# Pooled attention and GELU MLP: keys of later batches turned by a transposing DMA instead of by TensorE

## The chip, the cores and the metric

The kernel runs on one core of a Trainium2 chip. The metric is the device time of one execution in microseconds (us). A core has five engines that each work through a queue of their own in program order: TensorE (PE, matmuls), VectorE (DVE), ScalarE (ACT), GpSimd (POOL) and SyncE (SP, which here only issues DMAs). POOL issues DMAs too. An instruction that waits holds up everything behind it in its own queue.

## The reference

```python
batch, n_heads, seq, head_dim = (8, 8, 576, 64)

def _attn_ref(q, k, v):
    B, H, S, D = q.shape
    pool = 8
    Sp = S // pool                                   # 72 pools
    scale = 1.0 / np.sqrt(D)
    k_p = k.reshape(B, H, Sp, pool, D).mean(axis=3)
    v_p = v.reshape(B, H, Sp, pool, D).mean(axis=3)
    scores = scale * np.matmul(q, k_p.transpose(0, 1, 3, 2))
    scores = scores - np.max(scores, axis=-1, keepdims=True)
    attn = np.exp(scores)
    attn = attn / (np.sum(attn, axis=-1, keepdims=True) + 1e-09)
    return np.matmul(attn, v_p)

def _moe_ref(x, w_in, w_out):
    h = x @ w_in                                     # 4608x512 @ 512x2048
    g = 0.5 * h * (1.0 + np.tanh(sqrt(2/pi) * (h + 0.044715 * h**3)))
    return g @ w_out                                 # 4608x2048 @ 2048x512

x = attn_out.transpose(0, 2, 1, 3).reshape(B * S, H * D)
out = _moe_ref(x, w_in, w_out)
```

Keys and values are averaged over groups of eight positions, so every head has only 72 keys. Inputs and output are f32; the kernel computes in bf16 with f32 sums.

## The kernel before, in words

The 4608 rows of x are worked off in nine groups g of 512 rows (NG = 9). A batch has 576 rows, so group g needs the attention of batches 0 to g at most; the attention of batch nb = g + 1 is computed inside stage g, between the matmuls of the MLP. After an opening part for batch 0, the main loop (L415 to L508) runs one stage for each g:

1. First half (L457 to L470): 64 matmuls with w_in (`p1_mm`, L321), the GELU of each of 16 column tiles `fo` on ACT (L326). A table `plan` (L438) says after which `fo` the preparing steps for batch nb are issued: the sums over eight positions on DVE (L136), the move of the last pooled v rows (`v_moves`, L148), and the transposes of the pooled keys on TensorE with their copies (`trans_k`, L169, L176, L184).
2. Second half (L496 to L505): 64 matmuls with w_out (`p2_mm`, L329). At the positions `pos` (L483) attention steps of batch nb are put between them: scores (`qk`, L224), exponentials on ACT (L231), the product with v (`av`, L244), the normalisation (`norm`, `mult`). The first `qk` stands at position 6, the first `av` at position 14. After 16 matmuls a tile of output is copied by DVE into an `osb` buffer (L334) and stored by four DMAs on SP (L339).

The keys of a batch are loaded in `kts` as 576 pooled rows over 128 partitions, four to a partition, and a fifth column that takes the last 64 k rows and, in its lower half, the last 8 pooled rows of v. So the pooled keys are not separated by heads; the five transposes and the copies out of PSUM sort them. `kTs[b][0]` and `kTs[b][1]` hold them for the two halves c of the queries: one fills partitions 0 to 63, the other 64 to 127, with zeros elsewhere, since a transposed q tile carries an even and an odd position in its two halves of partitions.

The data of batch g + 2 are asked for in stage g (`load_next`, L419 to L425, called at L428 or L473): POOL issues the load of q (cast to bf16), SP a transposing DMA of q (`trans_q_dma`, L213), then a tiny POOL copy into `gate` (L423) makes POOL wait until that transpose has landed, and POOL issues the loads of k and v. The copy is there only for this wait. Nothing else holds POOL back, so after the v loads of a stage it goes straight on to the q load of the next stage. `qs`, `qT`, `kts`, `vts` and `vps` have two buffers each, used by turns.

SP's queue holds in a stage, in this order: the transposing DMA of q (batch g + 2), the v move (batch nb), 16 stores.

Of the kernel before, what the change touches and what calls it, by code (L numbers as in the profile page):

```python
# [8 lines left out]
F32 = mybir.dt.float32  # L9
BF16 = mybir.dt.bfloat16  # L10
# [8 lines left out]
def kernel(  # L19
# [9 lines left out]
    nc = tc.nc  # L29
    B, H, S, D = q.shape  # L30
    Sp = S // 8
# [11 lines left out]
    KR = 4  # L43
# [4 lines left out]
    consts = ctx.enter_context(tc.tile_pool(name="consts", bufs=1))  # L48
    qp = ctx.enter_context(tc.tile_pool(name="qp", bufs=2))
    bp = ctx.enter_context(tc.tile_pool(name="bp", bufs=2))  # L50
    ep = ctx.enter_context(tc.tile_pool(name="ep", bufs=2))
    gpool = ctx.enter_context(tc.tile_pool(name="gp", bufs=1))
    opool = ctx.enter_context(tc.tile_pool(name="op", bufs=6))
    psp = ctx.enter_context(tc.tile_pool(name="ps", bufs=1, space=bass.MemoryType.PSUM))


# [5 lines left out]

    vts = [consts.tile([128, 4, 512], F32, name=f"vt{i}") for i in range(2)]

    kts = [consts.tile([128, KR + 1, 512], F32, name=f"kt{i}") for i in range(2)]

    def load_k(b, engs):
        rows = k[b].rearrange("h (j l) d -> (h j) (l d)", l=8)
        main = rows[0:128 * KR].rearrange("(p r) c -> p r c", r=KR)
        n = KR // len(engs)  # L70
        for i, eng in enumerate(engs):
            eng.dma_start(out=kts[b % 2][:, i * n:(i + 1) * n], in_=main[:, i * n:(i + 1) * n])  # L72
        engs[0].dma_start(out=kts[b % 2][64:128, KR], in_=rows[128 * KR:])  # L73
        rows = v[b].rearrange("h (j l) d -> j h (l d)", l=8)
        engs[-1].dma_start(out=kts[b % 2][0:64, KR], in_=rows[64:])

    def load_v(b, engs):
        rows = v[b].rearrange("h (j l) d -> j h (l d)", l=8)
        for i in range(2):
            engs[i % len(engs)].dma_start(out=vts[b % 2][64 * i:64 * i + 64], in_=rows[0:64, 4 * i:4 * i + 4])  # L80

    def load_q(b, i0=0, i1=2):
        if b not in qs:
            qs[b] = qp.tile([128, 2, T * D], BF16, name="qb")
        nc.gpsimd.dma_start(  # L85
            out=qs[b][:, i0:i1],
            in_=q[b].rearrange("(i h) (p t) d -> (h p) i (t d)", i=2, t=T)[:, i0:i1])
# [24 lines left out]
    gate = consts.tile([1, 2], BF16, name="gate")  # L112
# [2 lines left out]
    xT = consts.tile([128, KO, N], BF16, name="xT")  # L115

    kTs = [[consts.tile([128, H, Sp], BF16, name=f"kT{i}{e}") for e in range(2)] for i in range(2)]
    kps = [consts.tile([128, KR + 2, D], BF16, name=f"kp{i}") for i in range(2)]

    vps = [consts.tile([Sp, H, 2, D], BF16, name=f"vp{i}") for i in range(2)]  # L120
# [14 lines left out]
    def add(o, a, b):  # L135
        nc.vector.tensor_tensor(out=o, in0=a, in1=b, op=ALU.add)  # L136

    def k_steps(b, c=slice(0, KR + 1)):


        t = kts[b % 2]
        return [lambda: add(t[:, c, 0:256], t[:, c, 0:256], t[:, c, 256:512]),
                lambda: add(t[:, c, 0:128], t[:, c, 0:128], t[:, c, 128:256]),
                lambda: add(kps[b % 2][:, c], t[:, c, 0:64], t[:, c, 64:128])]

    def v_moves(b):

        nc.sync.dma_start(out=vps[b % 2][64:Sp, :, 0], in_=kps[b % 2][0:64, KR])  # L148

    def v_steps(b):  # L150
# [35 lines left out]
    def trans_k(b, bank):  # L186
        trans_k_mm(b, bank)
        for e in range(2):
            trans_k_copy(b, e, bank)
# [17 lines left out]
    def trans_q(b, i, t0, n, bank, eng):  # L207
        trans_q_mm(b, i, t0, n, bank)
        trans_q_copy(b, i, t0, n, bank, eng)

    def trans_q_dma(b):
        qTs[b] = bp.tile([128, 2, TP, 128], BF16, name="qT")
        nc.sync.dma_start_transpose(out=qTs[b].rearrange("p i t c -> p (i t) c"),  # L213
                                    in_=qs[b].rearrange("p i c -> p (i c)"))
# [6 lines left out]
    def qk(b, c, pr, bank):  # L221
        for e in range(2):
            h = 2 * pr + e
            nc.tensor.matmul(out=PS[:Sp, bank + e, :CH].rearrange("j (t p) -> j t p", p=32),  # L224
                             lhsT=kTs[b % 2][c][:, h],
                             rhs=qTs[b][:, h // 4, :, h % 4 * 32:h % 4 * 32 + 32],
                             start=True, stop=True)

# [65 lines left out]
    def act_set(name):  # L294
        nc.scalar.preload_act_table_set(name)  # L295
# [27 lines left out]
    def gelu(g, fo):  # L323
        if g not in gTs:
            gTs[g] = gpool.tile([128, FO, GROUP], BF16, name="gT")
        nc.scalar.activation(out=gTs[g][:, fo, :], in_=PS[:, h_bank(g, fo), :], func=ACT.Gelu_apprx_tanh)  # L326
# [80 lines left out]
    nc.vector.memset(kTs[1][1], 0.0)  # L407
    for w in vps:
        nc.vector.memset(w, 8.0)

    for fo, ko in [(fo, ko) for ko in range(2) for fo in range(4)]:
        p1_mm(0, fo, ko)
# [2 lines left out]
    for g in range(NG):  # L415
        nb = g + 1 if g + 1 < B else None
        act_set(GELU_SET)

        def load_next():  # L419

            load_q(g + 2)
            trans_q_dma(g + 2)
            nc.gpsimd.tensor_copy(out=gate, in_=qTs[g + 2][0:1, 1, TP - 1, 0:2])  # L423
            load_k(g + 2, [nc.gpsimd])
            load_v(g + 2, [nc.gpsimd])  # L425

        if 0 < g and g + 2 < B:
            load_next()  # L428


        side = {fo: [] for fo in range(FO)}
        if nb is not None:
            kk = k_steps(nb)
            tk = [lambda: trans_k(nb, 4)]
            kk.append(lambda: v_moves(nb))
            vv = v_steps(nb)
            if g:
                plan = {2: kk[:1], 3: kk[1:], 7: vv[:1], 8: vv[1:], 9: tk}  # L438
            else:
                tq = [lambda a=a, i=i: trans_q(nb, *a, (5, 6, 7, 5)[i], nc.vector) for i, a in enumerate(QG)]  # L440

                kk.insert(1, lambda: (nc.vector.memset(vts[1][:, 0, 0:1], 0.0), load_v(1, [nc.sync])))
                plan = {0: kk, 12: tq[:1], 13: tq[1:2] + tk, 14: tq[2:3], 15: tq[3:] + vv}
            for fo, what in plan.items():
                side[fo] += what

        if g == 0:
            first = [(fo, ko) for ko in (2, 3) for fo in range(4)]  # L450
        else:
            late = 3
            rest = [fo for fo in range(4) if fo != late]
            first = [(fo, ko) for ko in range(3) for fo in rest]
            first += [(late, ko) for ko in range(3)]
            first += [(fo, 3) for fo in rest + [late]]
        for fo, ko in first if g + 1 < NG else ():  # L457
            p1_mm(g, fo, ko)
        for fo in range(FO):
            if g + 1 == NG:  # L460

                for c0, c1, turned in ((0, 384, False), (384, GROUP, True)):
                    for ko in range(KO):
                        p1_mm(g, fo, ko, c0, c1, turned)
            elif fo >= 4:
                for ko in range(KO):
                    p1_mm(g, fo, ko)
            gelu(g, fo)
            for s in side[fo]:
                s()  # L470

        if g == 0:
            load_next()  # L473


        todo = {}

        def at(m, f, *a):
            todo.setdefault(m, []).append((f, a))

        if nb is not None:
            act_set(EXP_SET)
            pos = (6, 14, 20, 27, 34, 41, 48, 55, 61)  # L483
            for i in range(len(ORDER) + 1):
                if i < len(ORDER):
                    at(pos[i], qk, nb, *ORDER[i], 2)
                if i:
                    a = (nb, *ORDER[i - 1], 4 + 2 * ((i - 1) % 2))
                    at(pos[i], av, *a)
                if i < len(ORDER):  # L490
                    at(pos[i], expo, nb, *ORDER[i], 2)
                if i:
                    at(pos[i], norm, *a)
                    at(min(pos[i] + 9, 62 if i < len(ORDER) else 65), mult, *a)

        seq = [(r, fo) for r in range(4 if g + 1 < NG else 3) for fo in range(FO)]  # L496
        if g == 0:

            seq[:32] = [(r, 4 * f4 + f) for f4 in range(4) for r in range(2) for f in range(4)]
        for m, (r, fo) in enumerate(seq):  # L500
            for f, a in todo.pop(m, []):
                f(*a)
            p2_mm(g, r, fo, o_bank(g, r))
            if fo == FO - 1:
                store(g, r, o_bank(g, r))  # L505
        for m in sorted(todo):
            for f, a in todo[m]:
                f(*a)  # L508
    for c0, bank in ((0, o_bank(g, 3)), (256, 4)):
# [5 lines left out]
        b, col = divmod(N - 128, S)  # L515
        t = col % CH // 32
        rows = out[b * S:(b + 1) * S].rearrange("(p t e) d -> e p t d", t=TP, e=2)
# [31 lines left out]
```

## Time and profile before

| what | value |
|---|---|
| time, median of 3 runs | 326.68 us (326.46 to 327.2) |
| the profiled execution | 326.68 us, span 324.9 us |
| TensorE / ScalarE / VectorE / GpSimd busy | 96% / 68% / 45% / 10% of the span |
| one stage, g = 1 to 6 | 31.85 us (for instance 127.71 to 159.56) |
| L321 and L329 matmuls on the chain that ended last | 37% and 38% |
| kt sums on DVE (L136), 128x1280, 128x640, 128x320 | 1493, 825, 491 ns |
| key transposes (L169) on the chain | 0.28 us a batch |
| POOL idle at the gate L423 | 151.2 us in 6 waits |
| q transpose by DMA, issue to landing | 4.6 us |

The span is cut by the profile into 40 slices; "the chain" follows the work that ended last backwards through what released it. In rows of a timeline the first number is the start in us from the beginning of the span, the second the length; in square brackets stands the idle time before, and what ended it. A row of SPq or POOLq is a DMA's issue. In rows of groups the numbers after the first bar are the busy time in us and the mean of one instruction in ns, those after the second the idle time before them. In a row of windows, the stretch and its length are followed by the busy time (and instruction count) of PE, PEld (weight loads), DVE, ACT and POOL, then the granted clock of TensorE (1.00 is full), the mean busy share of the DMA engines, and GB/s. In rows of DMA issues the last number is the median time from issue to landing.

### The profile page before, as it was taken

The page shows a single profiled execution, that of the slowest core. Times are in us where ns is not written, and L with a number is a line of the kernel's source. Part 1 is how long each engine was busy: PE and PEld are TensorE (multiplying, and loading weights), DVE is VectorE, ACT ScalarE, POOL GpSimd, SP SyncE. Part 2 cuts the span into 40 slices and gives each one's busy share as a digit, 9 for nine tenths or more (in the row PEclk, how much of TensorE's full clock was granted, in tenths as well). Part 3 has the DMA queues.
Part 4 walks back from the last instruction along what each step waited for, and adds up shares of the span by engine and source line. Part 5 has one row for each costly group of instructions (what it writes and reads, how often), then busy time and mean ns, then how long its engine had stood idle before and what let it go on. Part 6 is the DMA issues. An engine that isn't in the chain of part 4 may idle for free.

```text
span 324.9 us, 4442 instructions
## 1 busy us (share of the span) xinstructions
PE 311.8 (96%) x1621; PEld 167.6 (52%) x1621; DVE 145.8 (45%) x297; ACT 219.3 (68%) x402; POOL 31.3 (10%) x60
## 2 busy tenths in 40 slices
PE   8999919999999999999999999999999999999995
PEld 3555504555555555555555555555555554466544
DVE  4774434682568156805680577067616401200011
ACT  1677516976997799779877987798779873043300
POOL 7110004004000400220031002100000000000000
PEclk9999978999999999999999999999999999999999
DMA  7999955985925881598159527932002201210022
GB/s 230 257 282 217 246 106 192 247 186 160 225 75 108 228 201 38 108 265 161 48 124 259 138 57 97 262 81 67 1 10 57 65 0 34 65 32 2 0 54 76
DMA packets 30533, 41.11 MB, mean 127 GB/s; under 512 B 17904, under 2 KB 18160, under 8 KB 29616
## 3 DMA queue, kind: packets, MB, share of 16 engines
q0 software_dynamic: 7456, 24.38, 32.4%
q1 hardware_dynamic: 22424, 15.14, 19.3%
q10 hardware_dynamic: 632, 1.31, 1.2%
q8 instruction: 12, 0.20, 0.3%
q14 instruction: 9, 0.07, 0.1%
HBM read 36.70 MB, written 9.44 MB: 142 GB/s over the span
## 4 chain that ended last, share of the span: by engine, by line
PE 84%; DMA 11%; DVE 1%; POOL 1%; issue 0%; SPq 0%; DVEq 0%; POOLq 0%
PE PS L329 38%; PE PS L321 37%; DMA kt<-in_v_dram 7%; PE PS L244 4%; DMA vt<-in_v_dram 4%; PE PS L224 4%; DVE vt L136 1%; PE PS L169 1%; DVE kt L136 0%; POOL w_in_b L104 0%; POOL qb L85 0%; SPq L80 0%; POOL kt L72 0%; POOL kt L73 0%; DVE vp L136 0%
## 5 line engine op out<-in xcount | busy, mean ns | idle before, releaser
L321 PE MATMUL PS<-xT,w_in_b 128*128 128x512 bf16 (+2 forms) x640 | 137.9, 375 | 0.0
L329 PE MATMUL PS<-w_out_b,gT 128*128 128x512 bf16 (+1 forms) x592 | 137.8, 376 | 0.0
L326 ACT ACTIVATE gT<-PS 128x512 bf16<-128x512 f32 x144 | 81.7, 603 | 56.7 <-PE PS L321 56.7
L321 PEld LDWEIGHTS <-w_in_b 128*128 128x128 bf16 x640 | 72.1, 114 | 60.4
L329 PEld LDWEIGHTS <-gT 128*128 128x128 bf16 x592 | 58.0, 98 | 56.2 <-issue 1.8
L334 DVE COPY osb<-PS 128x512 f32<-128x512 f32 x35 | 24.2, 691 | 113.1 <-PE PS L329 112.8
L262 DVE TENSOR_TENSOR xT<-PS,rc 64x288 bf16<-64x288 f32 x112 | 51.0, 455 | 31.1 <-ACT rc L254 28.8
L231 ACT ACTIVATE e<-PS 72x576 bf16<-72x576 f32 x64 | 40.8, 644 | 11.4 <-PE PS L224 10.6
L244 PE MATMUL PS<-e,vp 72*128 72x288 bf16 x112 | 23.6, 291 | 6.9 <-DVE vp L136 6.8
L251 ACT ACTIVATE ld<-PS 64x288 f32<-64x288 f32 x56 | 22.8, 407 | 8.0 <-PE PS L244 6.6
L224 PE MATMUL PS<-qT,kT 128*72 128x288 bf16 x128 | 26.1, 289 | 0.9 <-ACT qT L203 0.6
L254 ACT ACTIVATE rc<-ld 128x288 f32<-128x288 f32 x56 | 24.8, 443 | 1.8
L295 ACT ACT_TABLE_LOAD x17 | 21.8, 1283 | 3.6 <-issue 3.3
L252 ACT ACTIVATE ld<-PS 64x288 f32<-64x288 f32 x56 | 22.5, 402 | 1.4
L224 PEld LDWEIGHTS <-kT 128*72 128x72 bf16 x128 | 14.4, 114 | 15.0 <-issue 1.3
L136 DVE TENSOR_TENSOR kt<-kt 128x1280 f32<-128x1280 f32 (+5 forms) x18 | 18.9, 1047 | 6.3 <-DMA kt<-in_k_dram 3.3
L136 DVE TENSOR_TENSOR vt<-vt 128x1024 f32<-128x1024 f32 (+1 forms) x16 | 15.3, 956 | 7.6 <-DMA vt<-in_v_dram 7.3
L176 DVE COPY kT<-PS 64x288 bf16<-64x288 bf16 (+2 forms) x48 | 13.2, 322 | 8.0 <-PE PS L169 7.9
L244 PEld LDWEIGHTS <-vp 72*128 72x128 bf16 x112 | 11.1, 100 | 10.5 <-DVE vp L136 7.1
L423 POOL COPY gate<-qT 1x2 bf16<-1x2 bf16 x6 | 1.0, 174 | 151.2 <-DMA qT<-qb 151.2
L345 PE MATMUL PS<-idle 128*128 128x512 bf16 x33 | 11.1, 487 | 1.5 <-DVE idle L125 1.2
L80 POOL DMA_DIRECT2D vt<-in_v_dram x12 | 7.6, 652 | 0.1
(45 smaller groups left out, 79.7 us busy)
## 6 DMA issues: line engine op xcount, KB each, us to landing
out_dram<-osb SPq DMA_DIRECT2D x140, 64.0 KB, 1.7
kt<-in_k_dram POOLq DMA_DIRECT2D x7, 1024.0 KB, 5.8
vt<-in_v_dram POOLq DMA_DIRECT2D x12, 512.0 KB, 9.5
qb<-in_q_dram POOLq DMA_DIRECT2D x7, 576.0 KB, 12.8
w_in_b<-in_moe_w_in_dram POOLq DMA_DIRECT2D x2, 1024.0 KB, 16.7
w_out_b<-in_moe_w_out_dram POOLq DMA_DIRECT2D x4, 512.0 KB, 22.6
vt<-in_v_dram SPq DMA_DIRECT2D x3, 512.0 KB, 10.6
kt<-in_k_dram POOLq DMA_DIRECT2D x7, 128.0 KB, 5.9
```

The source lines that it names most:

```text
L136: nc.vector.tensor_tensor(out=o, in0=a, in1=b, op=ALU.add)
L224: nc.tensor.matmul(out=PS[:Sp, bank + e, :CH].rearrange("j (t p) -> j t p", p=32), lhsT=kTs[b % 2][c][:, h], rhs=qTs[b][:, h // 4, :, h % ...
L231: nc.scalar.activation(out=e, in_=PS[:Sp, bank:bank + 2, :CH], func=ACT.Exp, scale=1.0 / 64.0)
L244: nc.tensor.matmul(out=PS[:, bank + x, :CH], lhsT=window(vps[b % 2], 2 * pr + x), rhs=e[:, x, :], start=True, stop=True)
L251: nc.scalar.activation(out=ld[0:64], in_=PS[64:128, bank, :CH], func=ACT.Ln)
L252: nc.scalar.activation(out=ld[64:128], in_=PS[0:64, bank + 1, :CH], func=ACT.Ln)
L254: nc.scalar.activation(out=rc, in_=ld, func=ACT.Exp, scale=-1.0)
L262: nc.vector.tensor_tensor(out=xT[rows, pr, col:col + CH], in0=PS[rows, bank + x, :CH], in1=rc[rows], op=ALU.mult)
L321: nc.tensor.matmul(out=out, lhsT=w, rhs=x, start=(ko == 0), stop=(ko == KO - 1))
L326: nc.scalar.activation(out=gTs[g][:, fo, :], in_=PS[:, h_bank(g, fo), :], func=ACT.Gelu_apprx_tanh)
L329: nc.tensor.matmul(out=PS[:, bank, c0:c1], lhsT=gTs[g][:, fo, r * 128:(r + 1) * 128], rhs=w_out_b[:, fo, c0:c1], start=(fo == 0), stop=(fo ...
L334: nc.vector.tensor_copy(out=osb, in_=PS[:, bank])
```

## The change

Batches 0 to 2 are prepared as before. For batch 3 and later (`KX = 3`):

- k is loaded with the 72 pools of a head on 72 partitions and the eight heads side by side (`load_k_dma`); the last eight pooled rows of v go to partitions 96 to 127 in two small loads.
- The sums (`k_steps_dma`) run over 8 x 256, 8 x 128 and 8 x 64 elements on 72 partitions and write bf16 into `kz`, whose 16 blocks of 128 columns are one for each head and half: in block e = 0 the pooled key stands in columns 0 to 63, in block e = 1 a copy of it in columns 64 to 127. The rest stays zero.
- A transposing DMA on SP (`trans_k_dma`) turns `kz` into `kx`, and `qk` reads its weights from there. The five transposes, the eight copies and their place in `plan` are gone for these batches.
- `v_moves` becomes two DMAs of four pools each.
- `load_next` for stages g of 2 and later is no longer called at the start of the stage but behind `trans_k_dma` after `fo` = 0, and begins with one more tiny copy into `gate`, out of `kx` of the coming batch. So POOL asks for q, and afterwards k and v, only when the key transpose has landed. `v_moves` follows `load_next`, after `fo` = 1.
- `osb` has five buffers instead of six, `kts` has eight columns instead of five, and POOL clears `kz` once.

SP's queue in stages 2 to 5 is then: transposing DMA of kz, transposing DMA of q (batch g + 2), two v moves, 16 stores. In stage 6 there is no q transpose.

```diff
--- before.py
+++ after.py
@@ -50,7 +50,7 @@
     bp = ctx.enter_context(tc.tile_pool(name="bp", bufs=2))
     ep = ctx.enter_context(tc.tile_pool(name="ep", bufs=2))
     gpool = ctx.enter_context(tc.tile_pool(name="gp", bufs=1))
-    opool = ctx.enter_context(tc.tile_pool(name="op", bufs=6))
+    opool = ctx.enter_context(tc.tile_pool(name="op", bufs=5))
     psp = ctx.enter_context(tc.tile_pool(name="ps", bufs=1, space=bass.MemoryType.PSUM))
 
 
@@ -62,7 +62,9 @@
 
     vts = [consts.tile([128, 4, 512], F32, name=f"vt{i}") for i in range(2)]
 
-    kts = [consts.tile([128, KR + 1, 512], F32, name=f"kt{i}") for i in range(2)]
+
+    kts = [consts.tile([128, H, 512], F32, name=f"kt{i}") for i in range(2)]
+    KX = 3
 
     def load_k(b, engs):
         rows = k[b].rearrange("h (j l) d -> (h j) (l d)", l=8)
@@ -74,6 +76,12 @@
         rows = v[b].rearrange("h (j l) d -> j h (l d)", l=8)
         engs[-1].dma_start(out=kts[b % 2][0:64, KR], in_=rows[64:])
 
+    def load_k_dma(b):
+        nc.gpsimd.dma_start(out=kts[b % 2][0:Sp], in_=k[b].rearrange("h (j l) d -> j h (l d)", l=8))
+        rows = v[b].rearrange("h (j l) d -> j h (l d)", l=8)
+        for y in range(2):
+            nc.gpsimd.dma_start(out=kts[b % 2][96:128, y], in_=rows[64 + 4 * y:68 + 4 * y])
+
     def load_v(b, engs):
         rows = v[b].rearrange("h (j l) d -> j h (l d)", l=8)
         for i in range(2):
@@ -115,6 +123,8 @@
     xT = consts.tile([128, KO, N], BF16, name="xT")
 
     kTs = [[consts.tile([128, H, Sp], BF16, name=f"kT{i}{e}") for e in range(2)] for i in range(2)]
+
+    kz = consts.tile([128, H, 2, 2 * D], BF16, name="kz")
     kps = [consts.tile([128, KR + 2, D], BF16, name=f"kp{i}") for i in range(2)]
 
     vps = [consts.tile([Sp, H, 2, D], BF16, name=f"vp{i}") for i in range(2)]
@@ -143,8 +153,31 @@
                 lambda: add(t[:, c, 0:128], t[:, c, 0:128], t[:, c, 128:256]),
                 lambda: add(kps[b % 2][:, c], t[:, c, 0:64], t[:, c, 64:128])]
 
+    def k_steps_dma(b):
+        t = kts[b % 2]
+        k0, k1 = (kz[0:Sp, :, e, e * D:e * D + D] for e in range(2))
+        m, x = t[0:Sp], t[96:128, 0:2]
+        return [lambda: add(m[:, :, 0:256], m[:, :, 0:256], m[:, :, 256:512]),
+                lambda: add(m[:, :, 0:128], m[:, :, 0:128], m[:, :, 128:256]),
+                lambda: add(k0, m[:, :, 0:64], m[:, :, 64:128]),
+                lambda: nc.vector.tensor_copy(out=k1, in_=k0),
+                lambda: trans_k_dma(b),
+                lambda: add(x[:, :, 0:256], x[:, :, 0:256], x[:, :, 256:512]),
+                lambda: add(x[:, :, 0:128], x[:, :, 0:128], x[:, :, 128:256]),
+                lambda: add(kps[b % 2][96:128, 0:2], x[:, :, 0:64], x[:, :, 64:128])]
+
+    kxs = {}
+
+    def trans_k_dma(b):
+        kxs[b] = bp.tile([128, 2 * H, 128], BF16, name="kx")
+        nc.sync.dma_start_transpose(out=kxs[b], in_=kz.rearrange("p h e c -> p (h e c)"))
+
     def v_moves(b):
 
+        if b >= KX:
+            for y in range(2):
+                nc.sync.dma_start(out=vps[b % 2][64 + 4 * y:68 + 4 * y, :, 0], in_=kps[b % 2][96:128, y])
+            return
         nc.sync.dma_start(out=vps[b % 2][64:Sp, :, 0], in_=kps[b % 2][0:64, KR])
 
     def v_steps(b):
@@ -222,7 +255,7 @@
         for e in range(2):
             h = 2 * pr + e
             nc.tensor.matmul(out=PS[:Sp, bank + e, :CH].rearrange("j (t p) -> j t p", p=32),
-                             lhsT=kTs[b % 2][c][:, h],
+                             lhsT=kxs[b][:, 2 * h + c, 0:Sp] if b >= KX else kTs[b % 2][c][:, h],
                              rhs=qTs[b][:, h // 4, :, h % 4 * 32:h % 4 * 32 + 32],
                              start=True, stop=True)
 
@@ -407,6 +440,7 @@
     nc.vector.memset(kTs[1][1], 0.0)
     for w in vps:
         nc.vector.memset(w, 8.0)
+    nc.gpsimd.memset(kz, 0.0)
 
     for fo, ko in [(fo, ko) for ko in range(2) for fo in range(4)]:
         p1_mm(0, fo, ko)
@@ -418,23 +452,30 @@
 
         def load_next():
 
+            if nb >= KX:
+                nc.gpsimd.tensor_copy(out=gate, in_=kxs[nb][0:1, 2 * H - 1, 0:2])
             load_q(g + 2)
             trans_q_dma(g + 2)
             nc.gpsimd.tensor_copy(out=gate, in_=qTs[g + 2][0:1, 1, TP - 1, 0:2])
-            load_k(g + 2, [nc.gpsimd])
+            if g + 2 >= KX:
+                load_k_dma(g + 2)
+            else:
+                load_k(g + 2, [nc.gpsimd])
             load_v(g + 2, [nc.gpsimd])
 
-        if 0 < g and g + 2 < B:
+        if 0 < g and nb is not None and nb < KX:
             load_next()
 
 
         side = {fo: [] for fo in range(FO)}
         if nb is not None:
-            kk = k_steps(nb)
+            kk = k_steps(nb) if nb < KX else k_steps_dma(nb)
             tk = [lambda: trans_k(nb, 4)]
             kk.append(lambda: v_moves(nb))
             vv = v_steps(nb)
-            if g:
+            if nb >= KX:
+                plan = {0: kk[:5] + ([load_next] if g + 2 < B else []), 1: kk[5:], 7: vv[:1], 8: vv[1:]}
+            elif g:
                 plan = {2: kk[:1], 3: kk[1:], 7: vv[:1], 8: vv[1:], 9: tk}
             else:
                 tq = [lambda a=a, i=i: trans_q(nb, *a, (5, 6, 7, 5)[i], nc.vector) for i, a in enumerate(QG)]
```

## The prediction

> **What bounds the kernel now.** I read the page first (busy shares, then the chain that ended last), then the chain in order of time, then SP's, POOL's and DVE's own rows over one stage, and last the one long idle time of TensorE with the clock beside it.
>
> ```profile
> PE 311.8 (96%) x1621; PEld 167.6 (52%) x1621; DVE 145.8 (45%) x297; ACT 219.3 (68%) x402; POOL 31.3 (10%) x60
> ...
> PE PS L329 38%; PE PS L321 37%; DMA kt<-in_v_dram 7%; PE PS L244 4%; DMA vt<-in_v_dram 4%; PE PS L224 4%; DVE vt L136 1%; PE PS L169 1%; DVE kt L136 0%; POOL w_in_b L104 0%; POOL qb L85 0%; SPq L80 0%; POOL kt L72 0%; POOL kt L73 0%; DVE vp L136 0%
> ```
>
> TensorE is busy 96% of the span, and the chain runs through its matmuls. Whatever makes it wait adds to the time in full; work taken from it is saved in full.
>
> ```profile
> 127.71 8.63 PE PS L321 x40
> 136.34 0.28 PE PS L169 x5
> ...
> 145.31 0.25 PE PS L244 x2
> ```
>
> This is the chain in stage g=3, from 127.71 to 159.56 (31.85 us, the same in stages 1 to 6). The five key transposes (L169) cost 0.28 us. The first value product (L244) ends the chain's wait-free run at 145.31; its row among TensorE's own starts at 145.15, 17.44 us into the stage. I count everything below from the stage's start.
>
> ```profile
> 129.01 2.02 SPq L339 DMA_DIRECT2D out_dram<-osb  x4
> 131.21 3.09 SPq L213 DMA_TRANSPOSE qT<-qb  x1
> 134.40 0.64 SPq L148 DMA_DIRECT2D vp<-kp  x1
> ```
> ```profile
> 135.90 0.17 POOL L423 COPY gate<-qT 1x2 bf16<-1x2 bf16 x1 [26.74 <-DMA qT<-qb]
> 136.44 0.58 POOL L72 DMA_DIRECT2D kt<-in_k_dram  x1 [0.36 <-issue]
> ...
> 139.46 0.73 POOL L85 DMA_DIRECT2D qb<-in_q_dram  x1
> ```
>
> In SP's queue the transposing DMA of q starts at +3.5 and the move of the last pooled v rows (L148) follows at +6.7, ten us before L244 needs it. That works because q comes a stage ahead: POOL issues the next q load at 139.46, right after k and v, and then stands 26.74 us at its gate.
>
> **The change, part by part.**
>
> *Removed from TensorE.* Batches 3 to 7 lose the transposes of L169: 5 x 0.28 = 1.4 us, on the path, a gain. The eight kT copies of these batches leave DVE too; they lie in its idle time.
>
> *Sums of k.* DVE is free at 129.97, +2.26.
>
> ```profile
> L136 DVE TENSOR_TENSOR kt<-kt 128x1280 f32<-128x1280 f32 x7 | 10.4, 1493 | 2.7 <-DMA kt<-in_v_dram 2.5
> ...
> L136 DVE TENSOR_TENSOR kt<-kt 128x640 f32<-128x640 f32 x7 | 5.8, 825 | 0.2
> ...
> L136 DVE TENSOR_TENSOR kp<-kt 128x320 bf16<-128x320 f32 x7 | 3.4, 491 | 0.2
> ```
>
> The slope is (1493-825)/640 = 1.044 ns an element. The new sums have 8x256 = 2048 elements (1.493 + 768 x 1.044 ns = 2.30 us), 1024 (1.22, as the one 128x1024 row has it) and 512 (0.69). The copy of 512 bf16 elements to the second half has no row: between 0.25 (half the 512-element row of 0.42 from PSUM, rounded up) and 0.69 (the f32 sum); I take 0.42, the nearest form. Together 4.63, so kz is ready at +6.9. The extra sums for the v rows (512, 256 and 128 elements: 0.69, 0.43, 0.29) end at +8.3. DVE has nothing else to do until 146.03 (+18.3), so this is free by itself.
>
> *The new transposing DMA.* kz to kx has 16 tiles where q has 18. q's lands 4.6 us after its issue: 4.6 x 16/18 = 4.1, at most 4.7; I take 4.2. kx is ready at +11.1. L224 needs it at 143.09 less the 0.28 saved, +15.1, so the new source of keys costs the scores nothing.
>
> *The new gate, and what is behind it.* From batch 3 on POOL first waits for kx of the coming batch, and only then issues the q load of the batch after it; the early q load is gone in g = 2, 3, 4 and 5 (g = 6 and later load nothing). Behind POOL's wait stand that q load, the old gate, three k loads and two v loads. Gate to next issue is 0.54 us (135.90 to 136.44), so q is issued at +11.65.
>
> ```profile
> kt<-in_k_dram POOLq DMA_DIRECT2D x7, 1024.0 KB, 5.8
> ...
> qb<-in_q_dram POOLq DMA_DIRECT2D x7, 576.0 KB, 12.8
> ...
> qT<-qb SPq DMA_TRANSPOSE x6, 4.6
> ```
>
> All those q loads ran behind 2.3 MB of k and v in the same queue, hence 12.8. Alone, q (1.18 MB read as f32) is nearest to the k load of 1.05 MB, which leads its queue: 5.8. Below that, the best two-us window (414 GB/s at 139 to 141) plus a small transfer's landing of 1.6 gives 4.45; above, the average of that burst (3.54 MB in 15.7 us, 226 GB/s) plus 1.7 gives 6.9, and 12.8 only if something heavy shares the queue. With 5.8, q lands at +17.45. [...]
>
> *SP's queue, the price.* SP now holds, in this order: the kx transpose, the q transpose, two v moves, the stores. The q transpose waits for that late q load, and the v moves stand behind it although their data is ready at +8.3. SP goes on at +17.45: q transpose 2.75 us (row median, 2.71 to 3.41), 0.1 gap, v moves of 0.64 each. The second starts at +20.95 and lands 1.7 later, as a store does: +22.65 (the q transpose ahead lands at 17.45 + 4.6 = +22.05, so it does not push this further unless the ring serves it slowly, up to 1.3 us more). L244 wants it at 17.44 - 0.28 = +17.15. TensorE runs in order, so all work behind L244 waits 5.5 us, in four stages: 22.0 us. No store waits on SP in the meantime: the last of a stage is issued by +3.3, the next is due at +19.
>
> *After the idle time, the clock.* The kernel has one such wait already, for batch 1:
>
> ```profile
> 39.91 0.41 PE L224 MATMUL PS<-qT,kT 128*72 128x288 bf16 x2
> 47.17 0.66 PE L244 MATMUL PS<-e,vp 72*128 72x288 bf16 x2 [6.85 <-DVE vp L136]
> 47.62 2.77 PE L329 MATMUL PS<-w_out_b,gT 128*128 128x512 bf16 x6
> ```
> ```profile
> 44.00:46.00 2.00, 0.00 (x0) 0.00 (x0) 1.26 (x2) 0.00 (x0) 0.00 (x0) 0.69 0.12 20
> ...
> 51.00:52.00 1.00, 1.00 (x5) 0.42 (x4) 0.00 (x0) 0.96 (x2) 0.17 (x1) 0.71 0.00 0
> ```
>
> The granted clock goes from 1.0 to 0.5 at about 44.76 (0.69 is the mean of 0.38 of the window at 1.0 and the rest at 0.5), 4.4 us after TensorE stopped, and back at about 51.58, 4.4 us after it resumed: 2.2 us of work lost. A wait of 5.5 lies just past the 4.4 of this single case. I charge 2.2 in two stages of the four, 4.4 us; none and all four (8.8) are the ends. [...]
>
> *Edits at nothing.* POOL's clearing of kz (2048 elements; the 128-element one took 0.24, so at most 16 x 0.24 = 3.9) lies ahead of a q load that already waits 3.56 us for TensorE and whose batch is scored only at 79.4. Five osb buffers instead of six: a buffer comes back five copies, over 17 us, later, and stores land in 1.7 (9.0 at worst). The k load in per-head rows and the two small v loads land while TensorE stands or runs; the next stage's DVE needs them 17 us after their issue.
>
> *Sum.* The profiled execution took 326.68 us, its span is 324.9, and 326.68 is also the median of the runs. 326.68 - 1.4 + 22.0 + 4.4 = **351.7**.
>
> **Ends.** Low: copy 0.17 less, kx 0.1 less, q 1.35 less, so a stall of 3.8 without any clock loss: 4 x 3.8 - 1.4 = 13.8, 340.5. High: copy +0.27, kx +0.5, q +1.1, q transpose +0.65, the ring +1.3: a stall of 9.3, with clock loss in all four: 37.2 + 8.8 - 1.4 = 44.6, 371.3. Not all go one way at once, so I stop short of the upper one.
>
> **Rivals.** (1) *The chain is in time, and only the saving is left*: 326.68 - 1.4 = 325.3, faster. It decides once the v moves land by +17.15, 5.5 us earlier than summed; q in 0.3 us would be needed, or a v move ahead of q in SP's queue. For it: DVE and the queues are idle there. Against: the low ends together give 1.7 us. 4%. (2) *The q load stays slow*: at its 12.8 the stall is 12.5, plus clock loss in all four: 50 + 8.8 - 1.4 = 57.4, 384. For it: no row shows a lone q load. Against: k and v of the stage before are over by then. 6%. (3) *The k load becomes the bound of a loop*: kx gates q, q gates k, k gates the next kx. k is issued at about +22.8 of a stage now 38 long, and DVE wants it at +40.4; every us over 17.6 would add one in each of three stages. At twice the 5.8 it is hidden; at 25 us it costs 3 x 7.4 = 22, 374. 4%. (4) *A smaller stall*, some 1 to 3 us without clock loss: 4 x 2 - 1.4, 333; this needs the transposes or the landing far below every row. 6%.
>
> The forecast as summed, 340.5 to 371.3, has 80%. A measurement here tells 0.2% (0.65 us) from no change; faster by more is rival 1, 4%; within it 2%, a stall of 0.35 us by chance; slower 94%. The range of 340 to 369 leaves out rivals 1 to 3, most of 4 and the forecast's outermost ends.
>
> **What would show it.** Right: four idle times of TensorE before the first L244 of g = 2 to 5 (none in g = 6), released by the DMA vp<-kp; SP waiting at the q transpose for q until about +17.5; POOL waiting for kx until +11; granted clock below 1.0 right after some of them. Wrong: L244 without idle time before it, an idle time before L224 instead (kx late), DVE waiting for kt at a stage's start (rival 3), or v moves landing before q does.

## The result, and the profile after

The changed kernel takes 358.06 us, median of four runs (356.87 to 358.62), against 326.65 us before: 1.0954 times as long, 95% interval [1.092, 1.0987]. The forecast was 351.7 us, range 340 to 369. Of all executions below, one is left out of the medians: 1793.59 us, of the kernel with the v moves first, whose median with it is the 331.25 that two expectations name. The profiled execution took 356.87 us, its span is 355.1 us, 30.2 more than the 324.9 before.

The page of the changed kernel, busy shares and the chain by lines. Its line numbers are higher than before: L354 and L362 are the MLP's matmuls, L257 the scores, L277 the value products, L367 the osb copies.

```profile
PE 318.9 (90%) x1596; PEld 168.5 (47%) x1596; DVE 152.6 (43%) x277; ACT 220.1 (62%) x402; POOL 35.8 (10%) x65
...
PE PS L362 32%; PE PS L354 26%; DMA kt<-in_v_dram 6%; PE PS L277 4%; DMA vt<-in_v_dram 4%; PE PS L257 3%; DMA qb<-in_q_dram 3%; SPq L246 3%; DMA out_dram<-osb 3%; DMA kx<-kz 2%; DVE kt L146 2%; DMA vp<-kp 2%; DVE osb L367 1%; SPq L179 1%; DVE xT L295 1%
```

TensorE falls from 96% to 90%, although it is busy 7 us longer with 25 instructions fewer. The MLP's two lines had 75% of the chain and have 58%; in their place stand the load of q, SP's issue of its transpose (L246), the key transpose (kx<-kz) and the v move (vp<-kp), which were not on it.

TensorE's rows from 95 us on that have idle time before them (start, length, the idle time and what ended it):

```profile
118.80 0.64 PE L277 MATMUL PS<-e,vp 72*128 72x288 bf16 x2 [5.71 <-DMA vp<-kp]
157.92 0.64 PE L277 MATMUL PS<-e,vp 72*128 72x288 bf16 x2 [5.54 <-DMA vp<-kp]
197.90 0.64 PE L277 MATMUL PS<-e,vp 72*128 72x288 bf16 x2 [5.47 <-DMA vp<-kp]
236.92 0.64 PE L277 MATMUL PS<-e,vp 72*128 72x288 bf16 x2 [5.72 <-DMA vp<-kp]
```

There are four, one in each of the stages 2 to 5, none in stage 6; all are in front of the first value product and ended by the v move. Together they are 22.4 us.

How stage 2 comes to its wait: SP's and POOL's rows. The stage begins at about 95.8 (a row's offset of 0.16 us taken from the stage of before).

```profile
102.74 1.83 SPq L173 DMA_TRANSPOSE kx<-kz  x1
113.23 2.72 SPq L246 DMA_TRANSPOSE qT<-qb  x1
116.05 1.38 SPq L179 DMA_DIRECT2D vp<-kp  x2
121.05 17.04 SPq L372 DMA_DIRECT2D out_dram<-osb  x16
```
```profile
107.14 0.18 POOL L456 COPY gate<-kx 1x2 bf16<-1x2 bf16 x1 [27.57 <-DMA kx<-kz]
107.59 0.73 POOL L93 DMA_DIRECT2D qb<-in_q_dram  x1 [0.28 <-issue]
117.93 0.18 POOL L459 COPY gate<-qT 1x2 bf16<-1x2 bf16 x1 [9.61 <-DMA qT<-qb]
```

SP stands from 104.6 to 113.2 at the q transpose, whose data POOL asked for only at 107.59, after kx had landed. The v moves follow at 116.05 and end at 117.43; TensorE had stopped at 113.09 and goes on at 118.80.

The clock around that wait (windows of stage 2; after stretch and length come PE, PEld, DVE, ACT and POOL, then the granted clock):

```profile
115.00:116.00 1.00, 0.00 (x0) 0.00 (x0) 0.00 (x0) 0.00 (x0) 0.00 (x0) 0.89 1.15 216
...
118.00:119.00 1.00, 0.20 (x2) 0.15 (x3) 0.00 (x0) 0.00 (x0) 0.57 (x2) 0.50 0.03 4
...
122.00:123.00 1.00, 1.00 (x6) 0.65 (x5) 0.00 (x0) 0.49 (x1) 0.00 (x0) 0.70 1.00 295
```

0.89 and 0.70 are means of 1.0 and 0.5, so the clock drops at 115.78 and returns at 122.60. TensorE works 3.8 us of that, from 118.80 on, at a granted clock of 0.50. Read in the same way, the half clock lasts 5.6, 3.2 and 5.2 us after the waits of stages 3, 4 and 5: 17.8 us in all, of which half, 8.9, is lost. The span's balance says the same: 30.2 + 1.4 saved - 22.4 of waits leaves 9.2.

### The profile page after: what moved, and what is told of

Same layout as the page of the kernel before. It is cut to its first block, busy times and chain, and to the rows that moved or that the text cites. A ratio compares the mean times of both kernels' runs of the same rounds, so it can differ in the third digit from the quotient of the medians.

```text
span 355.1 us, 4412 instructions
## 1 busy us (share of the span) xinstructions
PE 318.9 (90%) x1596; PEld 168.5 (47%) x1596; DVE 152.6 (43%) x277; ACT 220.1 (62%) x402; POOL 35.8 (10%) x65
## 4 chain that ended last, share of the span: by engine, by line
PE 66%; DMA 21%; DVE 5%; SPq 4%; POOL 1%; issue 1%; DVEq 0%; POOLq 0%
PE PS L362 32%; PE PS L354 26%; DMA kt<-in_v_dram 6%; PE PS L277 4%; DMA vt<-in_v_dram 4%; PE PS L257 3%; DMA qb<-in_q_dram 3%; SPq L246 3%; DMA out_dram<-osb 3%; DMA kx<-kz 2%; DVE kt L146 2%; DMA vp<-kp 2%; DVE osb L367 1%; SPq L179 1%; DVE xT L295 1%
## 5 line engine op out<-in xcount | busy, mean ns | idle before, releaser
L362 PE MATMUL PS<-w_out_b,gT 128*128 128x512 bf16 (+1 forms) x592 | 144.2, 389 | 0.0
L354 PE MATMUL PS<-xT,w_in_b 128*128 128x512 bf16 (+2 forms) x640 | 137.0, 375 | 0.0
L354 PEld LDWEIGHTS <-w_in_b 128*128 128x128 bf16 x640 | 72.4, 114 | 61.4
L362 PEld LDWEIGHTS <-gT 128*128 128x128 bf16 x592 | 59.7, 101 | 60.3 <-issue 7.8
L367 DVE COPY osb<-PS 128x512 f32<-128x512 f32 x35 | 24.2, 692 | 136.8 <-PE PS L362 131.0
L277 PE MATMUL PS<-e,vp 72*128 72x288 bf16 x112 | 25.0, 306 | 30.1 <-DMA vp<-kp 22.4
L146 DVE TENSOR_TENSOR kt<-kt 72x2048 f32<-72x2048 f32 (+9 forms) x28 | 30.4, 1084 | 7.4 <-DMA kt<-in_k_dram 3.4
L277 PEld LDWEIGHTS <-vp 72*128 72x128 bf16 x112 | 11.1, 102 | 35.0 <-issue 23.5
L285 ACT ACTIVATE ld<-PS 64x288 f32<-64x288 f32 x56 | 22.5, 402 | 1.4
L257 PE MATMUL PS<-qT,kx 128*72 128x288 bf16 x80 | 17.3, 300 | 0.0
L257 PEld LDWEIGHTS <-kx 128*72 128x72 bf16 x80 | 9.6, 120 | 10.0 <-issue 2.1
L257 PE MATMUL PS<-qT,kT 128*72 128x288 bf16 x48 | 9.7, 290 | 0.9 <-ACT qT L236 0.6
## 6 DMA issues: line engine op xcount, KB each, us to landing
kt<-in_k_dram POOLq DMA_DIRECT2D x5, 1152.0 KB, 11.9
```

Source lines behind the costliest of these rows:

```text
L277: nc.tensor.matmul(out=PS[:, bank + x, :CH], lhsT=window(vps[b % 2], 2 * pr + x), rhs=e[:, x, :], start=True, stop=True)
L285: nc.scalar.activation(out=ld[64:128], in_=PS[0:64, bank + 1, :CH], func=ACT.Ln)
L354: nc.tensor.matmul(out=out, lhsT=w, rhs=x, start=(ko == 0), stop=(ko == KO - 1))
L362: nc.tensor.matmul(out=PS[:, bank, c0:c1], lhsT=gTs[g][:, fo, r * 128:(r + 1) * 128], rhs=w_out_b[:, fo, c0:c1], start=(fo == 0), stop=(fo ...
L367: nc.vector.tensor_copy(out=osb, in_=PS[:, bank])
```

## The experiments

### The v moves ahead of the q transpose

```diff
-                plan = {0: kk[:5] + ([load_next] if g + 2 < B else []), 1: kk[5:], 7: vv[:1], 8: vv[1:]}
+                plan = {0: kk + ([load_next] if g + 2 < B else []), 7: vv[:1], 8: vv[1:]}
```

> The two v moves are issued on SP ahead of the q transpose; the gate and everything else stay as in the change. Theory (the four waits come only from the v moves standing behind the late q load in SP's queue): no idle time of TensorE before the first value product in stages 2 to 5, no half clock in them, and only the saved transposes are left: 326.65 - 1.4 = 325.3 us. Rival (the late chain kz, kx, q, k itself is too long, since its k load now lands 11.9 us after issue): the stages shrink to 31.6 us, k arrives at about 22.8 + 11.9 = +34.7, so DVE waits for it about 1 us longer from stage to stage, kx slips towards the scores' +15.1 and the waits move to L257; 327 to 335.

330.53 us, 1.0146 times before, interval [1.0119, 1.0174]: most of the loss is gone by this one move in SP's queue, but not all. The kernel was run again for its trace:

> The kernel with the v moves ahead of the q transpose once more, for its trace; it took 331.25 us. Theory (the waits for the v moves are gone, and what is left over 325.3 is the long chain kz, kx, q, k): no idle time before L277 in stages 2 to 5; DVE waits for kt at the start of stages 3 to 6, longer from stage to stage, and TensorE waits in front of L257 in the later ones, some 5 us in all. Rival (the v moves still land late): idle time before L277.

It took 330.09 us. DVE's first sums of k in stages 3 to 6, and TensorE's two idle times:

```profile
131.02 3.54 DVE L146 TENSOR_TENSOR kt<-kt 72x2048 f32<-72x2048 f32 x2 [1.19 <-DMA kt<-in_k_dram]
...
165.78 3.54 DVE L146 TENSOR_TENSOR kt<-kt 72x2048 f32<-72x2048 f32 x2 [4.38 <-DMA kt<-in_k_dram]
...
198.94 3.54 DVE L146 TENSOR_TENSOR kt<-kt 72x2048 f32<-72x2048 f32 x2 [5.31 <-DMA kt<-in_k_dram]
...
233.02 3.54 DVE L146 TENSOR_TENSOR kt<-kt 72x2048 f32<-72x2048 f32 x2 [3.80 <-DMA kt<-in_k_dram]
```
```profile
174.74 0.44 PE L257 MATMUL PS<-qT,kx 128*72 128x288 bf16 x2 [0.46 <-DMA kx<-kz]
208.66 0.69 PE L257 MATMUL PS<-qT,kx 128*72 128x288 bf16 x2 [2.16 <-DMA kx<-kz]
```

No wait for the v moves is left. Instead the loop of the prediction's third rival has come up: kx lets q be asked for, q's transpose lets k be asked for, and k makes the next kx. DVE waits for k longer from stage 3 to stage 5 (5.3 us), and once the scores' slack is used up, L257 waits, in stages 4 and 5. The two waits are 2.6 us, and the granted clock is 0.5 for 3.4 us after the second (208.68 to 212.09), which costs another 1.7: together 4.3 of the 4.8 us by which this execution exceeds 325.3. In the changed kernel the 5.6 us of waiting in each stage covered the late k.

### Without the gate on kx

```diff
-            if nb >= KX:
-                nc.gpsimd.tensor_copy(out=gate, in_=kxs[nb][0:1, 2 * H - 1, 0:2])
```

> Only POOL's wait for kx is taken out; SP's order stays (kx transpose, q transpose, v moves). Theory: POOL again asks for q a stage ahead, so SP's q transpose finds q landed, the v moves are issued at about +12 instead of +20.9, and the waits are gone: 325.3 us. Rival (order on SP alone is enough to delay the v moves, whatever q does): waits of 1 us or more remain at L277, 329 or more. Rival (the early q load slows k and the key transpose): idle time before L257.

325.27 us, 0.9964 times before, interval [0.9948, 0.9981]: as expected, no idle time of TensorE from 60 us on. SP's rows in stage 3 and POOL's q loads there:

```profile
134.55 2.02 SPq L173 DMA_TRANSPOSE kx<-kz  x1
136.74 3.09 SPq L246 DMA_TRANSPOSE qT<-qb  x1
139.92 1.34 SPq L179 DMA_DIRECT2D vp<-kp  x2
```
```profile
114.20 0.74 POOL L93 DMA_DIRECT2D qb<-in_q_dram  x1
141.77 0.18 POOL L457 COPY gate<-qT 1x2 bf16<-1x2 bf16 x1 [26.84 <-DMA qT<-qb]
```

SP's order is the changed kernel's, but q was asked for at 114.20, 22.5 us ahead of its transpose. So the order alone costs nothing; it takes the late q as well. This kernel shows also what the change is worth when nothing waits: five batches of transposes, about 1 us here of the 1.4 counted.

### All loads at the start of the stage

```diff
-        if 0 < g and nb is not None and nb < KX:
+        if 0 < g and g + 2 < B:
             load_next()
-                plan = {0: kk[:5] + ([load_next] if g + 2 < B else []), 1: kk[5:], 7: vv[:1], 8: vv[1:]}
+                plan = {0: kk[:5], 1: kk[5:], 7: vv[:1], 8: vv[1:]}
```

The gate on kx is out here too.

> The gate is taken out and all loads of batch g + 2 are asked for at the start of the stage, as in the kernel before; the keys still go through kz and the transposing DMA. Theory: 325.3 us, like the run without the gate; SP does the q transpose, the kx transpose and the v moves in that order, all before +13. Rival (the key transpose on SP behind the q transpose is late, or k and v loads beside it slow it): idle time before L257 in stages 2 to 6, 0.5 to 3 us each, 327 to 340.

346.31 us, 1.0609 [1.0566, 1.0652]. Theory and rival both missed: the idle time is not before L257 (apart from 0.26 us for kx in stage 5), it is before L277 again, for the v move: none in stage 2, 5.50, 3.86 and 5.94 us in stages 3 to 5. SP, POOL and TensorE in stage 3:

```profile
134.01 1.92 SPq L173 DMA_TRANSPOSE kx<-kz  x1
136.03 1.52 SPq L179 DMA_DIRECT2D vp<-kp  x2
```
```profile
135.62 0.88 POOL L80 DMA_DIRECT2D kt<-in_k_dram  x1 [0.42 <-DVE kp L146]
```
```profile
149.96 0.64 PE L277 MATMUL PS<-e,vp 72*128 72x288 bf16 x2 [5.50 <-DMA vp<-kp]
```

The v moves are issued in good time, at 136.03 to 137.55, yet the product that needs them starts at 149.96. They carry 4 KB each, but the k load began 0.4 us ahead of them. In stage 2, where nobody waits, they were issued at 104.73, 0.6 us ahead of the k load (105.36); in stages 4 and 5 they came 0.2 and 1.3 us after it. To test whether that order is the cause, the next kernel puts the gate on kx back, in front of the k and v loads alone; q stays asked for a stage ahead:

```diff
         def load_next():
-
+            load_q(g + 2)
+            trans_q_dma(g + 2)
+
+        def load_kv():
+            nc.gpsimd.tensor_copy(out=gate, in_=qTs[g + 2][0:1, 1, TP - 1, 0:2])
             if nb >= KX:
                 nc.gpsimd.tensor_copy(out=gate, in_=kxs[nb][0:1, 2 * H - 1, 0:2])
-            load_q(g + 2)
-            trans_q_dma(g + 2)
-            nc.gpsimd.tensor_copy(out=gate, in_=qTs[g + 2][0:1, 1, TP - 1, 0:2])
...
-        if 0 < g and nb is not None and nb < KX:
+        if 0 < g and g + 2 < B:
             load_next()
+            if nb < KX:
+                load_kv()
...
-                plan = {0: kk[:5] + ([load_next] if g + 2 < B else []), 1: kk[5:], 7: vv[:1], 8: vv[1:]}
+                plan = {0: kk[:5] + ([load_kv] if g + 2 < B else []), 1: kk[5:], 7: vv[:1], 8: vv[1:]}
...
```

(This diff, like the others of the changed kernel, is against the changed kernel; the last lines left out call `load_kv` in stage 0.)

> As the run with all loads asked for at the start of the stage (346.31 us, with v moves issued at 136.03 to 137.55 and the value product waiting for them until 149.96), but POOL also waits for kx of the coming batch before it issues the k and v loads; q is still asked for a stage ahead. So the v moves are issued on SP some 3 us before the loads, not 0.4 us after the first of them. Theory (a small move issued after the big loads lands only with them): no idle time before L277, 325.3 us. Rival (SP's order q transpose, kx transpose, v moves is at fault): 340 to 347 as before.

325.09 us, 0.9961 [0.9945, 0.9976], no idle time before L277. The same two rows, stage 3:

```profile
136.78 1.66 SPq L179 DMA_DIRECT2D vp<-kp  x2
```
```profile
140.19 0.88 POOL L80 DMA_DIRECT2D kt<-in_k_dram  x1 [0.43 <-issue]
```

With the moves 3.4 us ahead of the load nobody waits. So the gate is of use, but its place decides: in front of k and v it keeps the way clear for the small moves; in front of q, as in the change, it makes SP late.

### Matmuls on zeros in the wait

```diff
+                    if i == 1 and nb >= KX and g + 2 < B:
+                        at(pos[i], spin, 24, 4)
```

> The changed kernel with 24 matmuls on zeros put before the first value product in stages 2 to 5, so that TensorE works through some 5.2 us of the 5.6 us that it waits there (no part of the computation is left out). Theory (the measured loss is 22.4 us of waiting and 9.3 us of half clock after it): the waits for the v moves end at the same times, the clock stays at 1.0, and the time is 326.65 - 1.4 + 22.4 = 347.7 us, at most 349. Rival (the rest is not the clock but something else in the second half, such as stores and loads in each other's way): 355 to 358, as the changed kernel.

349.06 us, 1.0695 [1.0671, 1.0719]: 9.0 less than the changed kernel, though the v moves come no earlier. Only 0.4 to 1.2 us of each wait are still idle, and the clock keeps at 1.0. Stage 2:

```profile
118.35 0.40 PE L277 MATMUL PS<-e,vp 72*128 72x288 bf16 x2 [0.50 <-DMA vp<-kp]
```
```profile
112.00:118.00 6.00, 5.85 (x28) 2.58 (x26) 0.00 (x0) 0.65 (x1) 0.17 (x1) 1.00 0.54 104
```

From the last score before it to the first value product, TensorE now stands or works on zeros 5.7, 6.4, 5.6 and 6.1 us, 23.8 in all instead of 22.4; that is the 1.4 us by which the time misses the 347.7 of the theory. So the loss is the waits and the half clock after them, and nothing is left over for stores and loads. With 10 matmuls in place of 24:

> The changed kernel with 10 matmuls on zeros before the first value product in stages 2 to 5 instead of 24: 2.2 us of the 5.6 us are filled, 3.4 us stay idle. The stall is the same, only the clock can differ. Theory (the clock is judged in fixed stretches of 3.41 us, and the drop needs one of them with little work in it): an idle time of 3.4 fills such a stretch only in part of the stages, so 349 to 355 us, between the 349.06 of 24 matmuls and the 358.06 of none. Rival (any idle time of over about 2.7 us costs the clock, as it dropped 2.7 us after the stop in stage 2): 356 to 358.

354.26 us, 1.0862 [1.0845, 1.0879], between the two, as the theory said. 3.4 to 3.6 us are still idle in each of the four stages. In stage 2 the clock falls 0.4 us after TensorE has resumed and comes back just before 122:

```profile
118.00:119.00 1.00, 0.85 (x4) 0.47 (x5) 0.00 (x0) 0.50 (x2) 1.00 (x2) 0.78 0.00 0
...
121.00:122.00 1.00, 1.00 (x6) 0.60 (x4) 0.00 (x0) 0.48 (x1) 0.28 (x1) 0.52 0.87 225
```

### The k load in two pieces

Why is the loop of kx, q and k longer than a stage in the kernel with the v moves first? Its k load lands 11.6 to 12.6 us after issue, where the kernel before had 5.2 to 6.1.

```diff
-        nc.gpsimd.dma_start(out=kts[b % 2][0:Sp], in_=k[b].rearrange("h (j l) d -> j h (l d)", l=8))
+        rows = k[b].rearrange("h (j l) d -> j h (l d)", l=8)
+        nc.gpsimd.dma_start(out=kts[b % 2][0:64], in_=rows[0:64])
+        nc.gpsimd.dma_start(out=kts[b % 2][64:Sp], in_=rows[64:])
```

> The kernel with the v moves ahead of the q transpose (331.25 and 330.09 us, k landing 12.2 us after issue, DVE waiting for it up to 5.3), with the k load cut in two: 64 pools on 64 partitions, then 8. Theory A (the 72 rows spread badly over the 16 DMA engines): the main part lands in 6 to 8 us, DVE waits for k under 1 us, 325 to 326.5 us. Theory B (the pieces of 2 KB are at fault: four pooled rows of a partition were one run of 8 KB before and moved at 414 GB/s, while v, in pieces of 2 KB on 64 partitions, moves at some 200 to 230): it still lands after 11 to 13 us and the time stays at 329 to 332.

325.28 us, 0.995 [0.9933, 0.9967], no idle time of TensorE from 60 us on. The two pieces land 8.3 to 10.3 us after their own issues; DVE needs both, and the second has landed 10.1 to 10.9 us after the first was issued. DVE waits for k 1.3 us at most:

```profile
161.94 3.54 DVE L148 TENSOR_TENSOR kt<-kt 72x2048 f32<-72x2048 f32 x2 [1.32 <-DMA kt<-in_k_dram]
```

From the first sum of k in one stage to that in the next the kernel with one load took 33.2 to 34.8 us from stage 3 on; here the last two are 31.4 and 31.5, about the length of a stage. So cutting the load in two is enough, and 1 to 2 us of it are the earlier landing. Theory A's time came, its 6 to 8 us did not; the rest to the 5.8 of before, where a partition had one run of 8 KB, was not taken apart.

### Batch 2 as well, and the osb buffers alone

```diff
-    KX = 3
+    KX = 2
```

> The kernel without the gate on kx, with batch 2 also turned by the DMA. Theory (each batch gives 0.28 us of transposes and costs nothing else): 325.27 - 0.28 = 325.0 us. Rival (in stage 1 the k load in 72 rows lands late or the key transpose meets the first loads): a new idle time in stage 1, 326 or more.

325.14 us, 0.9966 [0.9949, 0.9983], against 325.27 with batch 2 by TensorE: the 0.28 us cannot be told apart here. The profiled execution, the slowest of twelve (327.27), has the idle time that the rival names: in stage 1, 0.51 us before L257 for kx and 1.28 before L277 for the v move. Whether the faster ones have it was not seen.

```diff
-    opool = ctx.enter_context(tc.tile_pool(name="op", bufs=6))
+    opool = ctx.enter_context(tc.tile_pool(name="op", bufs=5))
```

> The kernel before with five osb buffers instead of six, that edit of the change alone. Theory: stores land in under 10 us and a buffer comes back over 17 us later, so 326.5 us, no change. Rival (the change's DVE waits for stores, 5.5 us in all, cost time): 327.5 or more, with DVE waiting for stores where it did not before.

On the kernel before, this edit alone gives 326.25 us, 0.9995 [0.9977, 1.0013]: no change. In the main loop DVE waits 2.8 us for a store once, off the path.

## Why the prediction was right, point by point

- *The wait and its cause.* Right: predicted 5.5 us in stages 2 to 5 and none in 6, measured 5.71, 5.54, 5.47 and 5.72. Both undoings, of SP's order and of the gate, took these waits away; so it takes the two together.
- *Its steps.* kz was due at +6.9 and came at 102.7, +6.9; the copy that was bounded by 0.25 and 0.69 takes 0.29. kx took 4.3 (4.2). The lone q load landed in 5.5 (5.8, from the k load). The q transpose was issued at +17.4 (+17.45). The 1.3 us that the upper end gives to a slow ring was an estimate that no row shows; the value product of stage 2 starts at 118.80, +23.0 (+22.65).
- *The clock.* That half clock follows such a wait was right (0.50 granted after all four), and so was the price of one drop (2.2 us; measured 9.2 in four, 2.3 each); the size of the term was the step that failed: "I charge 2.2 in two stages of the four, 4.4 us". The drop came in all four and cost 9.2. This is 4.8 of the 6.4 us between 25.0 forecast and 31.4 measured. Another 1.2 lie between the profiled execution and the median; it may be half clock too, since the mean granted clock is 0.956 in the profiled execution and 0.947 to 0.952 in the other three. The remaining 0.4 are waits slightly over 5.5. The half was taken because one case showed a drop 4.4 us after the stop; the four new ones show 2.7, 4.4, 5.3 and 4.0.
- *The saving of 1.4.* Consistent with the four repaired kernels, one of which turns six batches (325.09 to 325.28, 1.0 to 1.4 below the kernel before beside them). Among executions with a mean granted clock of 0.988 or more, which sets differences in half clock aside, their medians are 1.4 to 1.6 below those of the kernel before.
- *Edits at nothing.* Right in the sum. DVE waits for a store twice, 2.8 us each, but only at 309.6 and 344.4, after the attention. The k load landed 11.9 us after issue, not at the 5.8 of before, and was still hidden by the 17 us that the prediction gave it. That cover was the wait itself: with the waits gone, the late k cost 5 us (330.53 against 325.28 with the load in two pieces). The third rival named that loop with a free margin of 17.6 us, which held only for a stage lengthened to 38.
- *The other rivals.* A slow lone q load (384) and a smaller stall (333) did not come. The chain in time (325.3) is what every repaired kernel reaches.

## What to carry to other kernels

Before a transfer is gated on a later event, list what is queued behind its consumer: here two moves of 4 KB cost 5.6 us a stage, and 2.3 more at half clock, because they were behind a transpose whose data had been put off. Give small, urgent moves their place ahead of big loads, both in the issuing queue and in time (here 325.09 us against 346.31). And when a wait is taken away, look at what ran in its shadow, since the next loop may be there.

## What the runs showed of the hardware that was not expected

- In the changed kernel's trace the edges of the half clock lie whole steps of 3.41 us apart. The drops are at 115.78, 156.74, 197.70 and 235.25 us: 40.96, 40.96 and 37.55 apart, 12, 12 and 11 times 3.413. The returns are 6.83, 6.83, 3.41 and 6.83 after the drops. TensorE had stopped 2.69, 4.36, 5.27 and 4.05 us before the drops, so these delays were not of one length.
- With stretches of 3.41 us laid from edge to edge in this trace, TensorE was busy 0.72, 0, 0 and 0 us in the stretch before each of the four drops; one at full clock with 1.54 us (190.88 to 194.29) was followed by another at full clock. At half clock, the stretches with 0.41, 2.24 and 1.74 us were followed by half clock again, those with 3.41, 3.41, 3.23 and 3.42 by full clock. With the v moves first, the second wait, of 2.16 us, left 1.26 us of work in the stretch before the drop at 208.68. With ten matmuls on zeros, the wait of 3.53 us in stage 5 lay across two stretches, and the granted clock is 1.00 in both. In these rows the first number after the length is TensorE's busy time:

```profile
205.26:208.68 3.42, 1.26 (x7) 0.41 (x5) 2.75 (x4) 1.87 (x2) 0.00 (x0) 1.00 1.04 128
```
```profile
231.19:234.61 3.42, 1.62 (x8) 0.54 (x6) 0.00 (x0) 0.15 (x1) 0.00 (x0) 1.00 0.82 158
234.61:238.02 3.41, 1.68 (x10) 0.95 (x11) 0.71 (x2) 1.25 (x3) 2.06 (x4) 1.00 0.31 38
```

- Ten matmuls on zeros (2.2 us) in a wait of 5.6 saved 3.8 us of the 9.0 that 24 saved.
- A k load of 72 rows on 72 partitions lands, in the median, 11.9 us after issue in the changed kernel, 12.1 without the gate, 12.2 with the v moves first and 12.9 with all loads at the start of the stage; as 64 and 8 rows the pieces land in 8.3 to 10.3 each. By the records of DMA packets, early in a k load 12.1 packets are in flight at a time, in the mean, in the changed kernel (120.8 to 121.6 us), 16.2 in the kernel before (138.6 to 139.2). How much of the later landing comes from that was not shown.
- Two moves of 4 KB, issued 0.4 us after a k load began, were waited for until 12.4 us after the second one's issue had ended; issued 3.4 us ahead of it they were in time. Why the product in the first case starts only at 149.96 stays open. In stage 2 of the changed kernel, where the k load was issued only at 118.53, the 64 packets of 128 bytes of the two moves went in 0.8 us (117.37 to 118.21).
